# Nyströmformer attention and a SiLU layer on one core: the scores of B and C as 32x32 array tiles

## The chip, the cores and the metric

The kernel runs on one core of one Trainium2 chip. The core has five engines with an instruction queue of their own each: TensorE (PE in the profile, its weight loads PEld), VectorE (DVE), ScalarE (ACT), GpSimd (POOL) and SyncE (SP); DMA queues move data beside them. The metric is the device time in microseconds of one execution, as the median of several runs. Before the change it is 289.93 us (three runs, 289.63 to 290.06).

## The reference

Eight batches, eight heads, 576 rows of 64 values. q and k are averaged over 18 rows each to 32 landmarks. Three softmax matrices follow: A (576x32, q against k's landmarks), B (32x32, landmarks against landmarks) and C (32x576, q's landmarks against k). Z is the inverse of B by six Newton-Schulz steps. The attention A Z C v goes through a layer with a SiLU.

```python
q_lm = q.reshape(B, H, m, S // m, D).mean(axis=3)      # m = 32
k_lm = k.reshape(B, H, m, S // m, D).mean(axis=3)
A = sm(q, k_lm)
Bm = sm(q_lm, k_lm)
C = sm(q_lm, k)
Z = Bm.transpose(0, 1, 3, 2) / (norm_1(Bm) * norm_inf(Bm) + 1e-06)
for _ in range(6):
    Z = 2 * Z - Z @ Bm @ Z
x = A @ Z @ C @ v           # then heads side by side: 4608 x 512
h = x @ w_in                # 512 x 2048
out = (h * sigmoid(h)) @ w_out
```

## The kernel before

The order on every engine is the order of the program text: a manual schedule, each engine executing its instructions in turn. An instruction that waits holds back all that stand behind it on its engine.

**Layout.** Heads go in two quads (g = 0, 1) of four heads; a head's 64 values are kept as 32 partitions times 2 (index e), so a quad fills 128 partitions, and each product with contraction over 64 values is two products (e = 0, 1) that add up. `nat` holds q and k as loaded, in four pieces j (0: q of quad 0, 1: k of quad 0, 2: q of quad 1, 3: k of quad 1), arriving in the order 1, 0, 3, 2. `transpose_qk` (L163, DVE) makes `qkT` of a piece. Landmark sums come from PE with the identity as weights (`landmarks_pe`, L170) for batches 0 to 2, and from five POOL additions (`landmarks_pool`, L183) later; `landmarks_out` (L177) copies PE's sums on ACT into `lmn`.

**Block-diagonal landmarks.** A dense product over 128 partitions mixes four heads, so the weights must be block-diagonal: `bd` (L146) is a 128x128 tile for each piece, zero outside four 32x32 blocks. Batches 0 and 1 (`tiled`) transpose the landmarks into the compact tile `lmc` (`lm_t`, L238), and `bd_expand` (L243) copies the blocks into `bd`. Batches from 2 on write the blocks with four DVE transposes and a fifth for the compact k landmarks `lmk` (`bdiag`, L224).

**Scores.** `b_scores` (L251): sixteen products on 32x32 array tiles from `lmc` in batches 0 and 1, four dense ones from `bd` and `lmk` later. `c_scores(g)` (L360): four dense products of 288 columns with `bd` into a two-bank PSUM tile `scp`. `c_max` (L368, DVE, a maximum and a scaling) and `c_exp` (L377, ACT) follow for each quad, `c_transpose` and `c_out` turn the result on PE in batches 0 and 1, a DMA transpose does it later; `w_scale` (L399) takes the reciprocal of C's row sums, `w_mm` (L405) multiplies with v. A's scores (`a_scores(i)`, L451, three pieces of rows) are dense products with `bd`; `a_max` (DVE) makes the maxima, `a_shift` (L480, PE) adds them to the scores in PSUM, `a_exp` (ACT) and `a_norm` (DVE, then POOL at L497) finish. B goes through `b_max`, `b_exp`, `b_norm` (its transpose `bmt` at L298), `f_mm`, `b_scale`, `f_out` and then `ns_mm` on PE and `ns_step` on DVE in turn, six Newton-Schulz rounds; `x_out`, `z_mm`, `z_out` and `m_unit` (four of them, 64x32 array tiles) give the layer's combined weights `mb`.

**Order.** The first batch's attention runs alone at the start (L597 to L677). Then the main loop goes over the batches: in step s of batch b, `l1(s)` makes layer 1 (four products into one of two two-bank PSUM buffers, the pool `psh`, which `scp` shares), `act(s)` is its SiLU on ACT, and `l2_mm(n)` issues n products of layer 2 from a queue of finished rows. The next batch's attention lies between these, from step d on: d is 6 in batch 0, 3 in batch 1 and 0 later. Step d (step 3 for batch 1) makes the block-diagonal tiles, step d+1 issues `b_scores`, `c_scores(0)` and their maxima, and step d+2 `c_scores(1)`, A's scores, `c_max(1)`, A's maxima, four l2 products, `a_shift(0)` and so on (L741 to L779). In batch 0 no l2 product is queued before step 8.

**Loads.** All loads are issued on POOL, in the order of the text, between POOL's own work; in the start the last w_out loads stand between the Newton-Schulz rounds (L645, L647), and w_in and the first two w_out before everything (L126 to L133).

Of the kernel before, what the change touches and what calls it, by code (L numbers as in the profile page):

```python
# [8 lines left out]
FP = mybir.dt.float32  # L9
BF = mybir.dt.bfloat16  # L10
AF = mybir.ActivationFunctionType
OP = mybir.AluOpType
AX = mybir.AxisListType

# [19 lines left out]
def kernel(  # L36
# [106 lines left out]

    bd_t = []
    for i in range(2):
        z = constp.tile([128, 4, 4 * L, 2], BF, tag=f"bd{i}", name=f"bd{i}")  # L146
        nc.vector.memset(z, 0.0)
        bd_t.append(z)

# [53 lines left out]
    class Att:  # L203
        def __init__(self, b):
            self.b = b
            self.qkT, self.v, self.lmn = qkT_t[b], v_t[b], lmn_t[b]
            self.bd = bd_t[b % 2]


            self.tiled = b < 2  # L210
            self.by_dma = b >= 2
            if self.tiled:
                self.lmc = attp.tile([128, 4, L, 2], BF, tag="lmc", name="lmc")
            else:
                self.lmk = attp.tile([128, 2, L, 2], BF, tag="lmk", name="lmk")
            self.bb = None
            self.m_done = 0
            self.csum = attp.tile([128, 2], FP, tag="csum", name="csum")
            self.eCT, self.t = [None, None], [None, None]
            self.s, self.sa, self.w = [None, None], [None] * 3, [None, None]  # L220
            self.fx = None


        def bdiag(self, gs=(0, 1)):  # L224
            j0, j1 = 2 * gs[0], 2 * gs[-1] + 2
            for h in range(4):
                p = slice(32 * h, 32 * h + 32)
                nc.vector.transpose(
                    out=self.bd[p, j0:j1, 32 * h:32 * h + 32, :]
                        .rearrange("p j l e -> p j (l e)").bitcast(FP),  # L230
                    in_=self.lmn[p, j0:j1, :].bitcast(FP))
            n = len(gs)
            nc.vector.transpose(
                out=self.lmk[:, gs[0]:gs[0] + n, :, :].rearrange("p g l e -> p (g l e)").bitcast(FP),
                in_=self.lmn.rearrange("p (g j) d -> p g j d", j=2)
                    [:, gs[0]:gs[0] + n, 1, :].bitcast(FP))

        def lm_t(self, g):  # L238
            nc.vector.transpose(
                out=self.lmc[:, 2 * g:2 * g + 2].rearrange("p j l e -> p (j l e)").bitcast(FP),  # L240
                in_=self.lmn[:, 2 * g:2 * g + 2, :].bitcast(FP))

        def bd_expand(self, g, *copy):  # L243
            for h in range(4):
                p = slice(32 * h, 32 * h + 32)
                copy[h % len(copy)](
                     out=self.bd[p, 2 * g:2 * g + 2, 32 * h:32 * h + 32, :],
                     in_=self.lmc[p, 2 * g:2 * g + 2])


        def b_scores(self):  # L251
            self.bb = psn1("bb")
            self.sb = self.bb[:, 448:512]
            if self.tiled:
                for g in range(2):
                    for e in range(2):
                        for h in range(4):
                            p = slice(32 * h, 32 * h + 32)
                            mm(self.sb[p, 32 * g:32 * g + 32], self.lmc[p, 2 * g, :, e],
                               self.lmc[p, 2 * g + 1, :, e], start=(g == 0 and e == 0),  # L260
                               stop=(e == 1))
                return
            for g in range(2):
                for e in range(2):
                    mm(self.sb[:, 32 * g:32 * g + 32], self.bd[:, 2 * g, :, e],
                       self.lmk[:, g, :, e], start=(g == 0 and e == 0), stop=(e == 1))

        def b_max(self):
            s2 = sc / (SEG * SEG)
# [87 lines left out]
            self.fx = n  # L357


        def c_scores(self, g):  # L360
            self.s[g] = ps2("scp")
            for hf in range(2):
                for e in range(2):
                    mm(self.s[g][:, hf, 0:HF], self.bd[:, 2 * g, :, e],
                       self.qkT[:, 2 * g + 1, HF * hf:HF * hf + HF, e],
                       start=(e == 0), stop=(e == 1))

        def c_max(self, g):  # L368
            mx = attp.tile([128, 1], FP, tag="cmx", name="cmx")
# [28 lines left out]

        def w_scale(self):  # L399
            self.wsc = attp.tile([128, 2], FP, tag="wsc", name="wsc")  # L400
            nc.vector.reciprocal(out=self.wsc, in_=self.csum)  # L401
            nc.vector.tensor_tensor(out=self.wsc, in0=self.wsc, in1=self.nrm, op=OP.mult)


        def w_mm(self):  # L405
            vv = self.v.rearrange("p h (c d) -> p h c d", d=Dh)
            self.w = psa1("wp")[:, 0:2 * Dh].rearrange("p (g d) -> p g d", d=Dh)
            for g in range(2):
                for c in range(VC):
                    for h in range(4):  # L410
                        p = slice(32 * h, 32 * h + 32)
                        mm(self.w[p, g, :], self.eCT[g][0:VP, c, p], vv[:, 4 * g + h, c, :],
                           start=(c == 0 and g == 0), stop=(c == VC - 1))

        def w_out(self):
# [35 lines left out]
        def a_scores(self, i):  # L451
# [8 lines left out]
            for c in range(2 * i, min(2 * i + 2, len(TCH))):  # L460
# [3 lines left out]
                for g in range(2):  # L464
                    for e in range(2):
                        mm(ov[:, g].rearrange("p r (j l) -> p r j l", l=L),
                           self.qkT[:, 2 * g, c0:c1, e],
                           self.bd[:, 2 * g + 1, :, e].rearrange("p (j r l) -> p r j l", r=2, l=L),
                           start=first, stop=(e == 1))
                        first = False  # L470

# [131 lines left out]
    a = Att(0)  # L603
    landmarks_pe(0, lp, 3, 1)
    a.lm_t(0)
    a.bd_expand(0, nc.scalar.copy)
    transpose_qk(0, 3)
    landmarks_pe(0, lp, 2, 1)
    transpose_qk(0, 2)
    landmarks_out(0, lp, 2, 2)  # L610
    a.lm_t(1)
    a.b_scores()
    a.bd_expand(1, nc.vector.tensor_copy, nc.scalar.copy)
    a.c_scores(0)
    a.b_max()
    a.b_exp()
    a.a_start()
    a.a_scores(0)
    a.c_max(0)
    a.c_exp(0)  # L620
    a.b_norm()
    a.f_mm()
    a.a_scores(1)
    a.b_scale()
    a.f_out()
    a.ns_mm()
    a.c_scores(1)
    a.a_max(0)
    a.ns_step()
    a.ns_mm()  # L630
# [4 lines left out]
    a.ns_mm()  # L635
    a.a_scores(2)
    a.a_shift(1)
    a.c_max(1)
    a.c_exp(1)
    a.a_exp(1)  # L640
    a.ns_step()
    a.ns_mm()
# [38 lines left out]
    for b in range(B):  # L681
# [14 lines left out]
        for s in range(NDC):  # L696
            if b > 1 and s in (0, 4) and a0.m_done < 4:
                a0.m_unit(a0.m_done)
            if b < 2 and s < 4:
# [13 lines left out]
                if b == 0 and s == 0:  # L713
# [1 line left out]
                    a0.a_out(1)  # L715
                    a = Att(1)
                    a.lm_t(0)
                    a.bd_expand(0, nc.gpsimd.tensor_copy)
                if s == 1 and b == 0:
                    landmarks_out(1, lp, 2, 2)  # L720
                    a.lm_t(1)
                    a.bd_expand(1, nc.gpsimd.tensor_copy)
                if s == 3 and b == 1:
                    landmarks_out(2, lp, 0, 4)
                    a = Att(2)
                    a.bdiag()
                l2_mm(cnt[s])
            elif b == 0 and s < 7:
                l1(s)
# [5 lines left out]

            elif s == d:
                l1(s)
                a.bdiag()
                act(s)
                l2_mm(cnt[s])  # L740
            elif s == d + 1:  # L741
                l1(s)
                a.b_scores()
                a.c_scores(0)
                a.b_max()
                a.c_max(0)
                act(s)
                table(AF.Exp)
                a.b_exp()
                l2_mm(cnt[s])  # L750
            elif s == d + 2:
                a.c_scores(1)
                a.a_start()
                a.a_scores(0)
                a.a_scores(1)
# [156 lines left out]
```

## Time and profile before

| | us |
|---|---|
| median of three runs | 289.93 |
| the profiled execution | 288.62 |
| its span in the profile | 286.4 |
| PE busy | 263.8 |
| ACT busy | 176.8 |
| DVE busy | 162.2 |
| POOL busy | 110.8 |
| layer 2 products (ops), 576 of them, busy | 148.1 |
| layer 1 products (hps), 512, busy | 83.0 |
| C's score products (scp), 64, busy | 12.1 |
| bdiag's transposes, 24 and 6 | 7.2 and 1.5 |

The span is what the profile records between the first and the last instruction of the execution; the time of a run has some 2.2 us around it. Products on PE overlap, so that busy times of groups are no sums of what each costs; two rows' starts show what lies between. The page's slices of PE's granted clock read 9 nearly throughout, with an 8 in slice 4 (from 21 us) and a 7 in slice 10 (from 64 us).

### The profile page before, as it was taken

What the parts mean: (1) busy time and instruction counts of PE and PEld (TensorE: products, weight loads), DVE (VectorE), ACT (ScalarE), POOL (GpSimd) and SP (SyncE); (2) the same over time, 40 slices, a digit from 0 to 9 for tenths busy, and PEclk for the clock granted to TensorE, in tenths of its full rate; (3) what the DMA queues carried; (4) which work ended last, traced back from release to release, by engine and by line L of the source; (5) the groups of instructions that cost most, each with busy time, mean ns of one, the idle gap of its engine ahead of it and who ended that gap; (6) DMA issues with size and microseconds to landing.
All of it is one profiled execution on the core that took longest, in us unless ns stands there. A gap on an engine that the chain in (4) does not pass through costs nothing.

```text
span 286.4 us, 6289 instructions
## 1 busy us (share of the span) xinstructions
PE 263.8 (92%) x2520; PEld 149.3 (52%) x2520; DVE 162.2 (57%) x396; ACT 176.8 (62%) x349; POOL 110.8 (39%) x139
## 2 busy tenths in 40 slices
PE   1787898997999899999899999999899999999994
PEld 1645555564554555455454655465545555456541
DVE  4896786376676754857676764856694652200000
ACT  2456686575756875669566865678566945646511
POOL 8335533213099409941597029710991030000000
PEclk9998999997999999999999999999999999999999
DMA  6999999916746874619494929203470603020012
GB/s 110 202 208 208 206 207 211 189 39 110 148 65 134 167 129 66 144 61 177 95 152 91 182 62 143 94 37 94 57 143 37 92 20 98 37 76 37 37 73 74
DMA packets 37788, 32.31 MB, mean 113 GB/s; under 512 B 18816, under 2 KB 29056, under 8 KB 37760
## 3 DMA queue, kind: packets, MB, share of 16 engines
q0 software_dynamic: 15104, 18.35, 39.4%
q1 hardware_dynamic: 22656, 13.57, 18.4%
q8 instruction: 19, 0.31, 0.5%
q14 instruction: 9, 0.07, 0.1%
HBM read 36.70 MB, written 9.44 MB: 161 GB/s over the span
## 4 chain that ended last, share of the span: by engine, by line
PE 76%; DVE 11%; POOL 5%; DMA 2%; ACT 2%; issue 1%; DVEq 0%; POOLq 0%; ACTq 0%
PE ops L72 40%; PE hps L72 18%; PE bb L72 5%; PE mp L72 4%; PE scp L72 3%; PE sa L72 3%; DMA nat<-in_q_dram 2%; DVE arec L495 2%; POOL lma L189 2%; PE lmp L72 1%; DVE fx L354 1%; DVE mb L538 1%; PE wp L72 1%; DVE cmx L370 1%; DVE arec L496 1%
## 5 line engine op out<-in xcount | busy, mean ns | idle before, releaser
L72 PE MATMUL ops<-w_out_sb,gT 128*128 128x512 bf16 x576 | 148.1, 382 | 0.1
L563 ACT ACTIVATE gT<-hps 128x576 bf16<-128x576 f32 x128 | 82.3, 650 | 60.0 <-PE hps L72 59.7
L72 PE MATMUL hps<-AT,mb 128*128 128x288 bf16 x512 | 83.0, 288 | 1.0 <-ACT gT L563 0.4
L72 PEld LDWEIGHTS <-gT 128*128 128x128 bf16 x576 | 51.9, 98 | 47.7 <-issue 6.5
L72 PEld LDWEIGHTS <-mb 128*128 128x128 bf16 x512 | 47.8, 98 | 27.0 <-issue 2.5
L497 POOL TENSOR_TENSOR an<-ex,arec 128x512 bf16<-128x512 bf16 (+1 forms) x24 | 21.4, 902 | 80.7 <-DVE wsc L401 38.3
L167 DVE STREAM_TRANSPOSE qkT<-nat 128x576 f32<-128x576 f32 x32 | 39.6, 1247 | 1.6 <-DMA nat<-in_k_dram 1.3
L538 DVE CAST mb<-mp 128x512 bf16<-128x512 f32 x32 | 22.1, 690 | 20.1 <-PE mp L72 19.7
L354 DVE SCALAR_TENSOR_TENSOR fx<-fx,bb 128x320 bf16<-128x320 bf16 (+2 forms) x48 | 18.3, 382 | 26.4 <-PE bb L72 26.2
L587 ACT COPY ost<-ops 128x512 f32<-128x512 f32 x36 | 21.0, 585 | 16.3 <-PE ops L72 15.2
L189 POOL TENSOR_TENSOR lma<-nat 128x1152 f32<-128x1152 bf16 x10 | 23.8, 2376 | 0.0
L140 ACT ACT_TABLE_LOAD x16 | 20.5, 1283 | 1.1 <-PEq L896 0.8
L539 ACT CAST mb<-mp 128x512 bf16<-128x512 f32 x32 | 18.7, 583 | 4.0 <-PE mp L72 4.0
L72 PEld LDWEIGHTS <-ident 128*128 128x128 bf16 (+1 forms) x240 | 12.3, 110 | 12.8 <-issue 5.3
L72 PE MATMUL lmp<-nat,ident 128*128 128x64 bf16 x216 | 11.0, 213 | 6.8 <-DMA nat<-in_k_dram 6.2
L72 PEld LDWEIGHTS <-fx 32*32 32x32 bf16 (+1 forms) x168 | 7.8, 95 | 16.1 <-DVE fx L354 7.3
L72 PE MATMUL bb<-fx 32*32 32x64 bf16 (+2 forms) x168 | 13.4, 211 | 2.9 <-DVE fx L354 2.5
L567 POOL COPY gT<-gT 128x1024 bf16<-128x1024 bf16 x4 | 4.1, 1036 | 30.0 <-ACT gT L563 30.0
L370 DVE TENSOR_REDUCE cmx<-scp 128x1 f32<-128x576 f32 x16 | 12.1, 757 | 4.9 <-PE scp L72 4.4
L495 DVE TENSOR_REDUCE arec<-ex 128x16 f32<-128x512 bf16 (+1 forms) x24 | 14.0, 585 | 0.0
L378 ACT ACTIVATE eC<-scp,cbs 128x576 bf16<-128x576 f32 x16 | 11.7, 740 | 3.6 <-DVE cbs L373 2.2
L488 ACT ACTIVATE ex<-sa 128x512 bf16<-128x512 f32 (+1 forms) x17 | 9.9, 584 | 6.2 <-PE sa L72 6.2
(82 smaller groups left out, 252.0 us busy)
## 6 DMA issues: line engine op xcount, KB each, us to landing
out_dram<-ost SPq DMA_DIRECT2D x36, 256.0 KB, 2.2
nat<-in_k_dram POOLq DMA_DIRECT2D x16, 288.0 KB, 6.2
nat<-in_q_dram POOLq DMA_DIRECT2D x16, 288.0 KB, 7.4
v<-in_v_dram POOLq DMA_DIRECT2D x8, 576.0 KB, 6.7
w_in_sb<-in_moe_w_in_dram POOLq DMA_DIRECT2D x4, 512.0 KB, 14.9
w_out_sb<-in_moe_w_out_dram POOLq DMA_DIRECT2D x4, 512.0 KB, 16.9
AT<-an SPq DMA_TRANSPOSE x30, 4.1
eCT<-eC SPq DMA_TRANSPOSE x12, 4.4
```

The lines of the kernel that those rows point to most:

```text
L72: nc.tensor.matmul(out=o, lhsT=lhsT, rhs=rhs, start=start, stop=stop, skip_group_check=True)
L140: nc.scalar.activation(out=spare[:, 1:2], in_=spare[:, 0:1], func=func)
L167: nc.vector.transpose(out=o.rearrange("p (l t) -> p t l", t=SEG), in_=nat_t[b][:, j, :].bitcast(FP).rearrange("p (t l) -> p t l", l=L))
L189: nc.gpsimd.tensor_tensor(out=a1, in0=nat[:, :, 0:3 * w], in1=nat[:, :, 3 * w:6 * w], op=OP.add)
L354: nc.vector.scalar_tensor_tensor(out=n[:, :, lo:], in0=self.fx[:, :, lo:], scalar=2.0, in1=self.p[:, :, lo:], op0=OP.mult, op1=OP.subtract)
L370: nc.vector.tensor_reduce(out=mx, in_=self.s[g][:, :, 0:HF], op=OP.max, axis=AX.XY, negate=True)
L495: nc.vector.tensor_reduce(out=r, in_=x, op=OP.add, axis=AX.X)
L497: nc.gpsimd.tensor_tensor(out=self.an[0:pr, c:c + n, :].rearrange("p c (h l) -> p (c h) l", l=L), in0=x, in1=r.unsqueeze(2).to_broadcast(( ...
L538: nc.vector.tensor_copy(out=o[:, 0, :], in_=m[0])
L539: nc.scalar.copy(out=o[:, 1, :], in_=m[1])
L563: nc.scalar.activation(out=gT_t[b][:, 2 * s:2 * s + 2, o:o + HF], in_=h[:, :, 0:HF], func=AF.Silu)
L587: nc.scalar.copy(out=ost, in_=st["ps"])
```

## The change

B's and C's scores use the compact landmarks `lmc` in every batch, on 32x32 array tiles. C's second quad writes its heads two quadrants away (`quadrant`: head h of quad 1 to partitions 32*(h^2)), and both quads' products are issued alternately, four and four. `bd` keeps only k's landmarks, for A, and is half as large. The rows of C in quad 1 being swapped by halves, `w_mm` reads `eCT` at the swapped place, and `w_scale` takes its reciprocals in three instructions. `bdiag` gives way to one `lm_t` over four pieces and four `bd_expand` copies on DVE.

The orders move too. In the loop, step d+1 now issues l1, act, l2, and then B's scores and both C quads, and step d+2 starts with A's scores. In the start, C's first quad with its maximum and exponential comes between the last two landmark sums; the last transpose (piece 2) moves from before B's scores to behind `f_mm`; `bd_expand` is half on POOL and half on ACT, behind `b_exp`; C's second quad, its maximum and its exponential come before B's norm and A's scores.

```diff
-        z = constp.tile([128, 4, 4 * L, 2], BF, tag=f"bd{i}", name=f"bd{i}")
+        z = constp.tile([128, 2, 4 * L, 2], BF, tag=f"bd{i}", name=f"bd{i}")
...
-        def bdiag(self, gs=(0, 1)):
...
-        def lm_t(self, g):
+        def lm_t(self, g, n=1):
             nc.vector.transpose(
-                out=self.lmc[:, 2 * g:2 * g + 2].rearrange("p j l e -> p (j l e)").bitcast(FP),
-                in_=self.lmn[:, 2 * g:2 * g + 2, :].bitcast(FP))
-
-        def bd_expand(self, g, *copy):
+                out=self.lmc[:, 2 * g:2 * g + 2 * n].rearrange("p j l e -> p (j l e)").bitcast(FP),
+                in_=self.lmn[:, 2 * g:2 * g + 2 * n, :].bitcast(FP))
+
+        def bd_expand(self, g, n, *copy):
             for h in range(4):
                 p = slice(32 * h, 32 * h + 32)
                 copy[h % len(copy)](
-                     out=self.bd[p, 2 * g:2 * g + 2, 32 * h:32 * h + 32, :],
-                     in_=self.lmc[p, 2 * g:2 * g + 2])
+                     out=self.bd[p, g:g + n, 32 * h:32 * h + 32, :],
+                     in_=self.lmc[p].rearrange("p (g j) l e -> p g j l e", j=2)[:, g:g + n, 1])
...
-                    mm(self.sb[:, 32 * g:32 * g + 32], self.bd[:, 2 * g, :, e],
-                       self.lmk[:, g, :, e], start=(g == 0 and e == 0), stop=(e == 1))
+                    for h in range(4):
+                        p = slice(32 * h, 32 * h + 32)
+                        mm(self.sb[p, 32 * g:32 * g + 32], self.lmc[p, 2 * g, :, e],
+                           self.lmc[p, 2 * g + 1, :, e], start=(g == 0 and e == 0),
+                           stop=(e == 1))
...
-        def c_scores(self, g):
-            self.s[g] = ps2("scp")
+        def quadrant(self, g, h):
+            h = h ^ (2 * g)
+            return slice(32 * h, 32 * h + 32)
+
+        def c_scores(self, gs=(0, 1)):
+            for g in gs:
+                self.s[g] = ps2("scp")
             for hf in range(2):
                 for e in range(2):
-                    mm(self.s[g][:, hf, 0:HF], self.bd[:, 2 * g, :, e],
-                       self.qkT[:, 2 * g + 1, HF * hf:HF * hf + HF, e],
-                       start=(e == 0), stop=(e == 1))
+                    for g in gs:
+                        for h in range(4):
+                            p = slice(32 * h, 32 * h + 32)
+                            mm(self.s[g][self.quadrant(g, h), hf, 0:HF],
+                               self.lmc[p, 2 * g, :, e],
+                               self.qkT[p, 2 * g + 1, HF * hf:HF * hf + HF, e],
+                               start=(e == 0), stop=(e == 1))
...
-            nc.vector.reciprocal(out=self.wsc, in_=self.csum)
+            nc.vector.reciprocal(out=self.wsc[:, 0:1], in_=self.csum[:, 0:1])
+            for r in range(2):
+                nc.vector.reciprocal(out=self.wsc[64 * r:64 * r + 64, 1:2],
+                                     in_=self.csum[64 - 64 * r:128 - 64 * r, 1:2])
...
     a.lm_t(0)
-    a.bd_expand(0, nc.scalar.copy)
+    a.c_scores((0,))
     transpose_qk(0, 3)
+    a.c_max(0)
+    a.c_exp(0)
     landmarks_pe(0, lp, 2, 1)
-    transpose_qk(0, 2)
     landmarks_out(0, lp, 2, 2)
     a.lm_t(1)
     a.b_scores()
-    a.bd_expand(1, nc.vector.tensor_copy, nc.scalar.copy)
-    a.c_scores(0)
+    a.c_scores((1,))
     a.b_max()
     a.b_exp()
+    a.bd_expand(0, 2, nc.gpsimd.tensor_copy, nc.scalar.copy)
+    a.c_max(1)
+    a.b_norm()
+    a.c_exp(1)
     a.a_start()
+    a.f_mm()
+    transpose_qk(0, 2)
     a.a_scores(0)
-    a.c_max(0)
-    a.c_exp(0)
-    a.b_norm()
-    a.f_mm()
-    a.a_scores(1)
     a.b_scale()
     a.f_out()
     a.ns_mm()
-    a.c_scores(1)
+    a.a_scores(1)
     a.a_max(0)
...
     a.a_shift(1)
-    a.c_max(1)
-    a.c_exp(1)
     a.a_exp(1)
...
-                    a.bdiag()
+                    a.lm_t(0, 2)
+                    a.bd_expand(0, 2, nc.vector.tensor_copy)
...
             elif s == d + 1:
                 l1(s)
+                act(s)
+                l2_mm(cnt[s])
                 a.b_scores()
-                a.c_scores(0)
+                a.c_scores()
                 a.b_max()
                 a.c_max(0)
-                act(s)
                 table(AF.Exp)
                 a.b_exp()
-                l2_mm(cnt[s])
             elif s == d + 2:
-                a.c_scores(1)
                 a.a_start()
```

In the loop, batch 1's `bd_expand` (two calls in steps 0 and 1 of batch 0) stays on POOL and copies one piece instead of two for each quad.

More of the change, by code (lines that the diff above doesn't have):

```diff
@@ L211, in __init__ @@
             self.by_dma = b >= 2
[L212 to L215, printed above, removed]
+            self.lmc = attp.tile([128, 4, L, 2], BF, tag="lmc", name="lmc")
             self.bb = None
@@ L221, in __init__ @@
             self.fx = None
-        def bdiag(self, gs=(0, 1)):
[L225 to L236, printed above, removed]
-        def lm_t(self, g):
-            nc.vector.transpose(
-                out=self.lmc[:, 2 * g:2 * g + 2].rearrange("p j l e -> p (j l e)").bitcast(FP),
-                in_=self.lmn[:, 2 * g:2 * g + 2, :].bitcast(FP))
-        def bd_expand(self, g, *copy):
+        def lm_t(self, g, n=1):
+            nc.vector.transpose(
+                out=self.lmc[:, 2 * g:2 * g + 2 * n].rearrange("p j l e -> p (j l e)").bitcast(FP),
+                in_=self.lmn[:, 2 * g:2 * g + 2 * n, :].bitcast(FP))
+        def bd_expand(self, g, n, *copy):
             for h in range(4):
@@ L253, in b_scores @@
             self.sb = self.bb[:, 448:512]
[L254 to L262, printed above, removed]
             for g in range(2):
                 for e in range(2):
-                    mm(self.sb[:, 32 * g:32 * g + 32], self.bd[:, 2 * g, :, e],
-                       self.lmk[:, g, :, e], start=(g == 0 and e == 0), stop=(e == 1))
+                    for h in range(4):
[3 more added lines that the diff above has]
+                           stop=(e == 1))
         def b_max(self):
@@ L411, in w_mm @@
                         p = slice(32 * h, 32 * h + 32)
-                        mm(self.w[p, g, :], self.eCT[g][0:VP, c, p], vv[:, 4 * g + h, c, :],
+                        mm(self.w[p, g, :], self.eCT[g][0:VP, c, self.quadrant(g, h)], vv[:, 4 * g + h, c, :],
                            start=(c == 0 and g == 0), stop=(c == VC - 1))
@@ L467, in a_scores @@
                            self.qkT[:, 2 * g, c0:c1, e],
-                           self.bd[:, 2 * g + 1, :, e].rearrange("p (j r l) -> p r j l", r=2, l=L),
+                           self.bd[:, g, :, e].rearrange("p (j r l) -> p r j l", r=2, l=L),
                            start=first, stop=(e == 1))
@@ L717 @@
                     a.lm_t(0)
-                    a.bd_expand(0, nc.gpsimd.tensor_copy)
+                    a.bd_expand(0, 1, nc.gpsimd.tensor_copy)
                 if s == 1 and b == 0:
@@ L721 @@
                     a.lm_t(1)
-                    a.bd_expand(1, nc.gpsimd.tensor_copy)
+                    a.bd_expand(1, 1, nc.gpsimd.tensor_copy)
                 if s == 3 and b == 1:
@@ L737 @@
                 l1(s)
-                a.bdiag()
+                if b > 1:
+                    a.lm_t(0, 2)
+                    a.bd_expand(0, 2, nc.vector.tensor_copy)
                 act(s)
```

## The prediction

> **What bounds the kernel now.** I read first the page's busy rows, then the chain that ended last, then the table of who waited for whom, and last the timeline of four places where this edit works: the start, and the changes to the second, third and seventh batch. In the first row TensorE is busy 263.8 of 286.4 us and no other engine passes 62%: from 27 us on, what makes PE wait or adds PE time is paid in full. The last three rows say where PE still waits.
>
> ```profile
> PE 263.8 (92%) x2520; PEld 149.3 (52%) x2520; DVE 162.2 (57%) x396; ACT 176.8 (62%) x349; POOL 110.8 (39%) x139
> ...
> PE lmp L72 <- DMA nat<-in_k_dram: 6.2, 2, 5.6
> PE bb L72 <- DVE lmk L233: 2.8, 2, 1.9
> PE bb L72 <- DVE fx L354: 2.5, 4, 0.9
> ```
>
> The timeline of the start (start, duration, engine, line, instruction, in brackets the idle time before and its releaser). Until about 27 us no layer 1 exists to fill PE: the path runs through landmarks, B's scores (bb<-lmc), B's norm, six Newton-Schulz rounds and z. POOL's rows are the other thing to see: it issues the loads in order, and each w_out issue waits for an earlier load to land.
>
> ```profile
> 10.21 1.12 PE L72 MATMUL lmp<-nat,ident 128*128 128x64 bf16 x18 [0.33 <-DMA nat<-in_q_dram]
> 11.37 0.27 ACT L180 CAST lmn<-lmp 128x128 bf16<-128x128 f32 x1 [1.40 <-PE lmp L72]
> 11.69 0.52 PE L72 MATMUL bb<-lmc 32*32 32x32 bf16 x16 [0.35 <-ACT lmn L180]
> 14.63 0.24 DVE L298 STREAM_TRANSPOSE bmt<-bm 128x64 bf16<-128x64 bf16 x1
> 16.20 0.29 PE L72 MATMUL bb<-fx 32*32 32x64 bf16 x8
> 18.99 0.74 POOL L122 DMA_DIRECT2D w_out_sb<-in_moe_w_out_dram  x1 [2.40 <-DMA w_in_sb<-in_moe_w_in_dram]
> 24.27 0.25 PE L72 MATMUL bb<-xb,W 128*64 128x64 bf16 x4 [1.05 <-DVE xb L286]
> ```
>
> The change to the third batch: DVE makes both block-diagonal tiles late, PE waits 1.91 us, and then four l2 products take 1.88 instead of the usual 1.02 us. The granted clock is 0.50 from 68 to 70 us and 0.79 from 70 to 72.
>
> ```profile
> 66.80 0.27 PE L72 MATMUL bb<-lmk,bd 128*128 128x32 bf16 x4 [1.91 <-DVE lmk L233]
> 67.42 1.88 PE L72 MATMUL ops<-w_out_sb,gT 128*128 128x512 bf16 x4
> 72.21 0.38 PE L72 MATMUL sa<-nm,ident 128*128 128x512 bf16 x1
> ```
>
> A later change (to the seventh batch): no wait, C's quads lie apart, four l2 products between them.
>
> ```profile
> 190.21 0.26 PE L72 MATMUL bb<-lmk,bd 128*128 128x32 bf16 x4
> 190.31 0.67 PE L72 MATMUL scp<-qkT,bd 128*128 128x288 bf16 x4
> 191.68 0.67 PE L72 MATMUL scp<-qkT,bd 128*128 128x288 bf16 x4
> 192.39 0.76 DVE L370 TENSOR_REDUCE cmx<-scp 128x1 f32<-128x576 f32 x1 [0.43 <-PE scp L72]
> 193.99 0.38 PE L72 MATMUL sa<-nm,ident 128*128 128x512 bf16 x1
> ```
>
> **The price of a tiled score.** A dense C quad costs PE 0.51 us (190.31 to the next product at 190.82), both 1.02; dense B costs 0.10 (190.21 to 190.31). Tiled B, at 36.92 us, holds PE 0.20 (sixteen products). Entering and leaving the tiled mode: a step with m_unit lasts 1.80 us (147.08 to 148.88 in the chain), one without 1.35 (125.88 to 127.23); of the 0.45, one stream of 512 columns is 0.215 (0.86 for four), so the two switches cost 0.235. Tiled C is 4 rounds of 8 products. If a round is one stream of 288 columns (0.12), C costs 0.48; if the quads don't overlap, 8 rounds, 0.96. m_unit runs eight products of 512 columns in that 0.215, so eight tiles over two PSUM banks do overlap; I take 0.55, with 0.07 for the last round's staggered starts. B and C thus cost 0.20 + 0.55 + 0.235 = 0.99 against 1.12: 0.13 gained, where nothing else waits.
>
> One rule speaks against that. Four heads of one quad write one bank here. The Newton-Schulz row has four heads in one bank too: its first result reaches DVE 0.29 us after the start (46.98 to 47.27), where one after the other the eight streams of 64 columns would alone need about 0.21 on top of the usual latency. The Trainium skill, TensorEngine Tiling (Array Packing), Gotcha 1: PSUM Pressure, says that different row tiles cannot use one bank at the same time. By that rule C would go two at a time, 16 x 0.12 = 1.92 us, about 1.4 more in each of seven stages, near 10 us on the sum; by the row it costs nothing, and I follow the row.
>
> **A stage of batches 3 to 6 (four of them).** Moved: act(s) and the four l2 products before B, both C quads together. Now from l1 (189.72) to the first a_shift (193.99) is 4.27, PE never idle. After: l1 0.48, l2 0.86, switch in 0.10, B 0.20, C 0.55 = 2.19. Then DVE takes two c_max in a row and a_max. The start of the second batch already shows this: cmx at 37.85, the next at 38.71, a_max 39.56, a_shift at 40.30, so 2.45 from the first c_max. The first c_max follows PE's last score by 0.20 (190.82 to 191.02). 2.19 + 0.20 + 2.45 = 4.84. PE itself needs only switch out 0.14, A's scores 0.92 and l2 0.88 = 1.94 of that 2.65, and stands 0.7 us at a_shift. Behind it in PE's queue lie the third A score, l2 and layer 1; nothing else is late there to take it up. Loss 0.55 a stage, 2.2 in all; bounds 0.48 (C at 0.48) and 0.98 (C at 0.96). On DVE five transposes (1.48) become one of about 0.3 and four copies of 0.18, all under PE's work; uncovered they would cost at most the 1.91 us that bdiag costs in the third batch. The second batch's POOL copies (four of 0.29 for each quad, now half as wide) lie under layer 1; uncovered, 1.2 us.
>
> **Third batch.** DVE ends its transposes at 65.25, lm_t is done at 65.55. PE: l1 64.23, l2 to 65.57, B from 65.67: the 1.91 us wait is gone, so I take the clock's fall as gone too (a wait of 0.87 at 95.53 brought none, and the new stall is 0.9). Expansion ends about 66.3, then b_max, c_max from 66.75, a_shift 66.75 + 2.45 = 69.2 against 72.21: gain 3.0. Bounds 1.9 (the wait alone) and 3.9 (no stall). **Fourth batch.** The 0.87 us wait goes: l1 to a_shift was 5.30 (94.01 to 99.31), becomes 4.84: gain 0.5. **Second batch.** act(7) has no l2 to hide it: C's second quad needs its buffer, free at 37.75; 37.75 + 0.55 + 0.20 + 2.45 = 40.95 against 40.30: loss 0.6.
>
> **The start.** (a) C's first quad is set between the last two landmark sums; products there are slow (scp x4 1.14 at 12.14, 0.67 at 190.31), so PE is busy with it from 9.8 to about 11.0 and the last landmarks end 12.1 instead of 11.33. (b) ACT's copy of them now queues behind c_exp(0), which waits for c_max(0): 11.1 + 0.95 + 0.95 = 13.0, so B's scores start at 13.6 instead of 11.69, 1.9 late. (c) From there to bmt one C quad lies in between, as before: bmt ends 16.8. (d) The last transpose_qk, idle time at 10.20 before, now stands between b_norm and b_scale: 1.26, then the same 1.24 (14.91 to 16.15): f_out at 19.3. (e) Half of bd_expand goes to POOL, and in POOL's order behind the w_out issue at 18.99, paced by loads: 18.99 + 0.74 + two copies of 0.29 = 20.35. A's first scores wait for it, and the first Newton-Schulz product stands behind them on PE: 20.4 + 0.9 = 21.3 against 16.20, 5.1 late. (f) From there to z the old 8.07 us lose a C quad's c_max (0.86) on DVE and c_exp on ACT; A's second scores take the C quad's place on PE. I take 0.7 off: z comes 4.4 late. Bounds: 5.1 (nothing off) and 1.3: without (e) 1.9 + 1.26 - 0.7 = 2.5, less 1.2 if the spell at clock 0.64 (27 to 31 us) goes, in which four hps took 1.37 instead of 0.66 and eighteen landmark products 1.17 instead of 0.69. Three reciprocals for one in w_scale: 2 x 0.15, within that. The smaller memsets end before the first load lands.
>
> **Sum.** 4.4 + 0.6 - 3.0 - 0.5 + 2.2 = +3.7 us. The profiled execution took 288.62 us (span 286.4 and 2.2 around it) and lies 1.3 under the median of 289.93: 292.3 there, 293.6 as a median.
>
> **Rivals.** Quads that run one after the other: 0.41 more in seven stages, +2.9: 296.5. For it: no row shows two different moving operands in one head's row strip with weights changed every round; against it m_unit. 0.10. POOL's copies not held: only (e) falls, start 2.5 late, sum +1.8: 291.7; for it, POOL has nothing but issues there, against it the order of its queue. 0.15, of which 0.05 ends within no change. The other side: DVE's chain doesn't hold a_shift. Then a stage is 2.19 + 1.94 = 4.13, gain 0.14 x 4, third batch 3.9, fourth 1.2, second 0.3 lost: 4.4 + 0.3 - 3.9 - 1.2 - 0.6 = -1.0: 288.9. It decides as soon as the stall falls from 0.7 below 0.1; for it, the first quad's products come first in each round; against it, 2.45 was measured. 0.15. That the edit does not do what it says I count as the first rival.
>
> **How the numbers follow.** Mine has 0.60: 293.6, own range 291.5 (c_max and c_exp both off the start's 5.1: 3.5; third batch 3.9; stages 0.48) to 295.4 (start 5.1, third batch 1.9). Faster by over 0.2% (about what a measurement of this kernel can tell from no change) is the last rival, 0.15; within it 0.05; slower 0.80. The range runs from 290.0 (the POOL rival, 291.7, less the clock's 1.2 and 0.07 for C in seven stages) to 296.8, just past the first rival; the last rival alone, and what lies beyond 296.8, stay out.
>
> **What would show it.** Right: bb<-fx first at 21 us, sa<-bd first at 20.4 released by POOL, ops at 65 us with no half clock, PE idle 0.7 before sa<-nm in late stages, the waits on lmk gone. Wrong: a first bb<-fx before 19, no such idle time, or scp taking 0.9 us of PE a batch.

## The result and the profile after

The changed kernel takes 300.76 us as the median of four runs (298.23 to 301.68), the kernel before 289.78 us in four runs (286.77 to 290.06): a ratio of 1.0387, 95% interval 1.0328 to 1.0446. It is slower by 11 us where the forecast said 3.7, and lies outside the range of 290.0 to 296.8. The profiled execution took 301.68 us with a span of 300.0, against 288.62 and 286.4; it is the slowest of the four, so that what is accounted for below is 13.9 us and not 11.

The busy row of the page and the head of the table of who waited for whom, by PE (total, times, longest, in us):

```profile
PE 262.9 (88%) x2748; PEld 148.1 (49%) x2784; DVE 163.8 (55%) x410; ACT 176.4 (59%) x345; POOL 110.9 (37%) x141
```

```profile
PE bb L76 <- DVE fx L336: 8.4, 8, 1.9
PE lmp L76 <- DMA nat<-in_k_dram: 6.7, 2, 5.6
PE sa L76 <- DVE nm L470: 4.4, 7, 0.8
PE sa L76 <- POOL bd L234: 4.0, 1, 4.0
```

PE is busy 0.9 us less in a span 13.6 us longer. Busy time is not work, though: up to step 8 of batch 0 PE is busy 36.4 us where it was 31.4, because its products take longer there ("Wrong, second step" below), and from there on 226.5 where it was 232.4. The wait on lmk is gone as forecast. Two waits were forecast, sa on POOL's bd and sa on DVE's nm (0.5 to 0.8 in seven stages). The largest one was not: bb on fx, 8.4 us, was 2.5.

To find where each microsecond went, I compared the start of every layer 1 step (hps) in the two profiled executions. The difference after minus before grows like this:

| place | forecast | measured |
|---|---|---|
| first layer 1 | +4.4 | +7.03 |
| from there to step 7 of batch 0 | 0 | +2.23 |
| change to the second batch | +0.6 | +0.53 |
| third | -3.0 | -3.09 |
| fourth | -0.5 | -0.56 |
| fifth to eighth, together | +2.2 | +1.89 (0.46 to 0.48 each) |
| a later step in each of batches 1 to 6 | 0 | +5.87 (six times 0.98) |
| sum | +3.7 | +13.9 |

The terms of the stages stand. Two things are wrong: the start, and a loss that the forecast doesn't have, always five steps behind the new scores.

**The stages as they are now.** The timeline at the third batch (start, duration, engine, line, instruction; in brackets the idle time before and its releaser), and at the seventh:

```profile
75.47 0.23 PE L76 MATMUL bb<-lmc 32*32 32x32 bf16 x9
78.94 0.38 PE L76 MATMUL sa<-nm,ident 128*128 128x512 bf16 x1 [0.80 <-DVE nm L470]
```

```profile
200.71 0.65 PE L76 MATMUL hps<-AT,mb 128*128 128x288 bf16 x4
202.16 0.47 PEld L76 LDWEIGHTS <-lmc 32*32 32x32 bf16 x48 [0.42 <-issue]
202.28 0.67 PE L76 MATMUL scp<-qkT,lmc 32*32 32x288 bf16 x28
202.88 1.10 PE L76 MATMUL sa<-bd,qkT 128*128 128x128 bf16 x16
203.00 0.76 DVE L362 TENSOR_REDUCE cmx<-scp 128x1 f32<-128x576 f32 x1
203.87 0.75 DVE L362 TENSOR_REDUCE cmx<-scp 128x1 f32<-128x576 f32 x1
205.45 0.38 PE L76 MATMUL sa<-nm,ident 128*128 128x512 bf16 x1 [0.61 <-DVE nm L470]
```

At the third batch B's scores follow layer 2 without a wait. At the seventh, B and both C quads, 48 products, hold PE from 202.16 to 202.88, and DVE's first c_max starts 0.12 later. From l1 to a_shift it is 4.74 us (200.71 to 205.45; forecast 4.84, before 4.27), with PE idle 0.61 at the end (forecast 0.7) behind two c_max and a_max.

**The start.** The timeline:

```profile
13.61 0.49 PE L76 MATMUL bb<-lmc 32*32 32x32 bf16 x12 [1.07 <-ACT lmn L184]
16.44 0.24 DVE L280 STREAM_TRANSPOSE bmt<-bm 128x64 bf16<-128x64 bf16 x1
19.51 0.74 POOL L126 DMA_DIRECT2D w_out_sb<-in_moe_w_out_dram  x1 [1.47 <-DMA w_in_sb<-in_moe_w_in_dram]
20.25 0.64 POOL L234 COPY bd<-lmc 32x128 bf16<-32x128 bf16 x2
20.94 1.01 PE L76 MATMUL sa<-bd,qkT 128*128 128x128 bf16 x8 [3.97 <-POOL bd L234]
21.89 0.29 PE L76 MATMUL bb<-fx 32*32 32x64 bf16 x8
30.66 0.47 PE L76 MATMUL bb<-xb,W 128*64 128x64 bf16 x4
```

POOL's two copies do stand behind the w_out issue, which waits for an earlier load, and A's first scores wait 3.97 us for them. The first Newton-Schulz product comes at 21.89 against 16.20: 5.69 late (forecast 5.1). From there to z it is 8.77 us where it was 8.07, and from z to the first layer 1 3.39 where it was 2.75.

**The loss that was not forecast.** The same place on either side, DVE's and POOL's rows around w_scale; the kernel before first, then the changed one:

```profile
78.73 0.25 DVE L496 RECIPROCAL arec<-arec 128x16 f32<-128x16 f32 x1
78.90 0.11 DVE L401 RECIPROCAL wsc<-csum 128x2 f32<-128x2 f32 x1
79.04 0.16 DVE L402 TENSOR_TENSOR wsc<-wsc,nrm 128x2 f32<-128x2 f32 x1
79.13 1.04 POOL L497 TENSOR_TENSOR an<-ex,arec 128x512 bf16<-128x512 bf16 x1 [10.99 <-DVE wsc L401]
80.00 0.43 DVE L354 SCALAR_TENSOR_TENSOR fx<-fx,bb 128x320 bf16<-128x320 bf16 x1
```

```profile
85.43 0.25 DVE L491 RECIPROCAL arec<-arec 128x16 f32<-128x16 f32 x1
85.60 0.10 DVE L393 RECIPROCAL wsc<-csum 128x1 f32<-128x1 f32 x1
85.72 0.33 DVE L395 RECIPROCAL wsc<-csum 64x1 f32<-64x1 f32 x2
85.83 1.04 POOL L492 TENSOR_TENSOR an<-ex,arec 128x512 bf16<-128x512 bf16 x1 [7.84 <-DVE arec L491]
86.08 0.81 DVE L397 TENSOR_TENSOR wsc<-wsc,nrm 128x2 f32<-128x2 f32 x1
87.69 0.43 DVE L336 SCALAR_TENSOR_TENSOR fx<-fx,bb 128x320 bf16<-128x320 bf16 x1
88.17 0.31 PE L76 MATMUL bb<-fx 128*128 128x160 bf16 x2 [1.06 <-DVE fx L336]
```

A multiply of 128x2 numbers takes 0.16 us before and 0.81 after. Before, it starts 0.09 us ahead of POOL's a_norm multiply, which arec has released (the row names wsc, but POOL starts 0.15 us behind the end of arec in both kernels). After, the two added reciprocals put it 0.25 us behind, and it ends where POOL's ends (86.89 and 86.87). The next ns_step on DVE starts 2.01 us behind the end of arec instead of 1.02, and PE, which did not wait there before, waits 1.06. The multiply's start is 0.34 us later and its length 0.65 more, together the 0.98 that the table has six times.

### The profile page after: what moved, and what is told of

The parts are those of the page before. It is cut to its first block, busy times and chain, and to the rows that moved or that the text cites. A ratio compares the mean times of both kernels' runs of the same rounds, so it can differ in the third digit from the quotient of the medians.

```text
span 300.0 us, 6795 instructions
## 1 busy us (share of the span) xinstructions
PE 262.9 (88%) x2748; PEld 148.1 (49%) x2784; DVE 163.8 (55%) x410; ACT 176.4 (59%) x345; POOL 110.9 (37%) x141
## 4 chain that ended last, share of the span: by engine, by line
PE 72%; DVE 15%; DMA 5%; issue 3%; ACT 2%; POOL 2%; POOLq 0%; DVEq 0%; ACTq 0%
PE ops L76 36%; PE hps L76 19%; PE bb L76 5%; DMA w_in_sb<-in_moe_w_in_dram 5%; PE mp L76 4%; DVE cmx L362 3%; DVE arec L490 3%; PE sa L76 2%; PE lmp L76 2%; DVE fx L336 2%; DVE wsc L397 2%; PE wp L76 1%; DVE nm L470 1%; PE scp L76 1%; DVE mb L533 1%
## 5 line engine op out<-in xcount | busy, mean ns | idle before, releaser
L76 PE MATMUL ops<-w_out_sb,gT 128*128 128x512 bf16 x540 | 140.9, 380 | 3.6 <-issue 2.4
L76 PE MATMUL hps<-AT,mb 128*128 128x288 bf16 x512 | 84.7, 292 | 0.8 <-DVE mb L533 0.3
L76 PEld LDWEIGHTS <-mb 128*128 128x128 bf16 x512 | 48.5, 99 | 27.9 <-issue 2.5
L76 PEld LDWEIGHTS <-ident 128*128 128x128 bf16 (+1 forms) x240 | 13.6, 117 | 13.8 <-issue 5.6
L76 PE MATMUL lmp<-nat,ident 128*128 128x64 bf16 x216 | 12.4, 225 | 7.0 <-DMA nat<-in_k_dram 6.7
L76 PEld LDWEIGHTS <-qkT 128*128 128x128 bf16 (+1 forms) x160 | 10.2, 104 | 14.3 <-issue 14.1
L76 PE MATMUL mp<-w_in_sb,zwT 64*32 64x512 bf16 x256 | 14.0, 414 | 0.0
```

Source lines behind the costliest of these rows:

```text
L76: nc.tensor.matmul(out=o, lhsT=lhsT, rhs=rhs, start=start, stop=stop, skip_group_check=True)
```

## The experiments

Offsets below are, as in the table, the start of a layer 1 step in the profiled execution less that of the kernel before. The kernels of 1 to 4, of 5 to 8 and of 9 to 11 each share their runs of the kernel before; ratios are to it, with 95% intervals.

**1. One reciprocal again.**

```diff
-            nc.vector.reciprocal(out=self.wsc[:, 0:1], in_=self.csum[:, 0:1])
-            for r in range(2):
-                nc.vector.reciprocal(out=self.wsc[64 * r:64 * r + 64, 1:2],
-                                     in_=self.csum[64 - 64 * r:128 - 64 * r, 1:2])
+            nc.vector.reciprocal(out=self.wsc, in_=self.csum)
```

> The changed kernel with w_scale's three reciprocals put back to one; the swap of the halves in the second quad's scales is left out. Theory A (collision): in the changed kernel the small multiply of w_scale takes 798 ns in the median instead of 161 because the two extra reciprocals (0.16 us each) let it start after POOL's multiply of a_norm has begun. Without them it takes about 160 ns again, PE's waits on fx of about 1 us in each of batches 1 to 6 go, and the kernel is 5.9 us (6 x 0.98) faster than the changed one, near 295. Theory B (the longer stage before it makes DVE late): the waits stay but for the 0.3 us of the two reciprocals, at most 1.9 us faster, 299 or more. The start stays 7.0 us late by both.

295.58 us, ratio 1.0151 [1.0122, 1.0180]. The row of the tile wsc (least, median and longest duration in ns):

```profile
L394 DVE TENSOR_TENSOR wsc<-wsc,nrm x8: 160/161/162, 28.1 to 239.0; 128x2 f32<-128x2 f32 x8
```

All six steps of 0.98 are gone (offset at the end 7.63 instead of 13.89); the start is unchanged at 7.03.

**2. The reciprocals kept, w_scale moved ahead of a_norm(0).**

```diff
                 if s == d + 4:
-                    a.a_norm(0)
                     a.w_scale()
+                    a.a_norm(0)
                     a.a_norm(1)
```

> The changed kernel with w_scale, three reciprocals and all, moved ahead of a_norm(0) in the main loop, so that its multiply ends before POOL's a_norm multiply can begin. Theory A (collision): the multiply is short again, DVE is later by 0.6 us a batch instead of 1.3; waits on fx fall from about 1 us to 0.3 or less, 4 to 5.9 us faster than the changed kernel. Theory B (the number of instructions on DVE counts, wherever they stand): same time as the changed kernel within 1 us.

296.03 us, ratio 1.0181 [1.0121, 1.0240]. The multiply's median is 161 ns again with all three reciprocals in place, and the step costs 0.34 a batch instead of 0.98. So the reciprocals' own time is a third of the loss and the meeting with POOL two thirds. This execution, whose start is the same (6.99), has no further loss up to step 7 (6.95): the 2.23 us of the changed kernel's table there are not in every execution.

**3. The kernel before, with its reciprocal cut in three and nothing else.**

```diff
-            nc.vector.reciprocal(out=self.wsc, in_=self.csum)
+            nc.vector.reciprocal(out=self.wsc[:, 0:1], in_=self.csum[:, 0:1])
+            for r in range(2):
+                nc.vector.reciprocal(out=self.wsc[64 * r:64 * r + 64, 1:2],
+                                     in_=self.csum[64 * r:64 * r + 64, 1:2])
```

> The kernel before, with w_scale's reciprocal in three instructions of the same sizes as in the change (no swap). Theory A (collision): its multiply starts 0.34 us later, after POOL's a_norm multiply has begun, and takes some 0.8 us in batches 1 to 6; 0.98 us lost in each, 5.9 us slower than before, near 295.7. Theory B (the stage order is to blame): 0.3 us of DVE work in batches in which DVE was not late, 0 to 1 us slower.

296.45 us, ratio 1.0178 [1.0147, 1.0210]: five us by two small instructions in a kernel without any of the change's scores. The timeline and the tile:

```profile
81.25 1.04 POOL L500 TENSOR_TENSOR an<-ex,arec 128x512 bf16<-128x512 bf16 x1 [11.01 <-DVE arec L499]
81.38 0.92 DVE L405 TENSOR_TENSOR wsc<-wsc,nrm 128x2 f32<-128x2 f32 x1
83.59 0.31 PE L72 MATMUL bb<-fx 128*128 128x160 bf16 x2 [1.06 <-DVE fx L354]
```

```profile
L405 DVE TENSOR_TENSOR wsc<-wsc,nrm x8: 160/915/931, 23.4 to 238.6; 128x2 f32<-128x2 f32 x8
```

Again the multiply starts inside POOL's row and ends with it (82.30 and 82.29), and 0.98 is lost in each of six batches. Another 2.1 us are lost at the start.

**4. The old order of the start in the changed kernel** (all of the diff's lines of the first batch undone, with C's quads as tiles in their old places).

```diff
-    a.c_scores((0,))
+    a.bd_expand(0, 1, nc.scalar.copy)
...
-    a.bd_expand(0, 2, nc.gpsimd.tensor_copy, nc.scalar.copy)
...
-    a.ns_mm()
-    a.a_scores(1)
+    a.ns_mm()
+    a.c_scores((1,))
```

> The changed kernel with the first batch's order as it was before (C's quads at their old places, the last transpose ahead of B, bd_expand on ACT and DVE for each quad when its landmarks are there), scores still tiled. Theory: the new order of the start costs 7.0 us up to the first layer 1 product, and the slow products until 44 us another 2.2; the old one gives all of it back: 9 us faster than the changed kernel, near 291.5. Rival: tiled products themselves are slow in the start, or the load order paces it: less than 4 us come back. In the trace the first layer 1 product starts at 27 us by the theory and after 31 by the rival.

295.93 us, ratio 1.0184 [1.0137, 1.0230]. The first layer 1 is 0.10 late instead of 7.03: the start's loss is the new order's. The spell behind it, in which products run at about half their rate, did not go: 1.9 us more are lost by step 4 of batch 0 (the kernel before has such a spell too, with a granted clock of 0.57 from 26 to 30 us; here it is 0.50 from 26 to 34). With experiment 1 this accounts for the result, within the intervals: 1.0387 less the 0.0236 that experiment 1 takes off and the 0.0203 of this one is 0.995.

**5. The new start, with POOL's copies given to ACT.**

```diff
-    a.bd_expand(0, 2, nc.gpsimd.tensor_copy, nc.scalar.copy)
+    a.bd_expand(0, 2, nc.scalar.copy)
```

> The changed kernel with all four bd_expand copies of the first batch on ACT, none on POOL. Theory: A's first scores and behind them the first Newton-Schulz product wait 4.0 us for POOL's two copies, which queue behind two paced w_out issues; on ACT they wait for the last transpose alone (about 18.0 us): A's first scores 2.9 us earlier than 20.94, the first layer 1 product near 31 instead of 34.05, about 3 us faster than the changed kernel, near 297. Rival: DVE's chain (transpose, B's scale) sets the end anyway: less than 1 us.

297.90 us, ratio 1.0270 [1.0214, 1.0326]. A's first scores start at 16.16, the first Newton-Schulz product at 18.17 instead of 21.89, and the first layer 1 is 3.30 late: 3.7 of the 7.0 us are POOL's queue.

**6. The fifth kernel, with the transpose back at its old place.**

```diff
     landmarks_pe(0, lp, 2, 1)
+    transpose_qk(0, 2)
     landmarks_out(0, lp, 2, 2)
...
     a.f_mm()
-    transpose_qk(0, 2)
```

> The same, and the last transpose of the first batch back at its old place, ahead of the landmarks' copy. Theory: its 1.26 us leave the path between B's norm and its scale; the first Newton-Schulz product comes 1.2 us earlier than with the copies on ACT alone, the first layer 1 product near 30, some 2.8 us after that of the kernel before: what is left is the landmarks' copy queued on ACT behind C's first exponential (1.9 us) and C's quad on PE. Near 296. Rival: A's scores, which need this transpose, hold the path at the same place: no gain over the copies on ACT alone.

298.32 us, ratio 1.0248 [1.0168, 1.0328]; the first layer 1 is 2.89 late, 0.4 better where 1.2 was expected. The transpose behind f_mm was nearly free: back in its old place it holds up lm_t(1), and B's scores start at 13.37 instead of 12.86. In the profiled execution a later loss of 1.64 us, where the granted clock fell to 0.56 behind a wait of 1.91 us on fx, hides the gain; the medians of the two experiments can't be told apart.

**7. Three more layer 2 products ahead of the first a_shift, in the changed kernel**, to fill the 0.6 us in which PE waits for nm.

```diff
-                l2_mm(4)
+                l2_mm(7)
                 a.a_shift(0)
...
-                l2_mm(cnt[s] - 6)
+                l2_mm(cnt[s] - 9)
```

(The table of counts gives step d+2 three more and three later steps one less each.)

> The changed kernel with three more l2 products ahead of the first a_shift in each stage, taken from steps 8 to 10 of the batch. Theory: PE stands 0.6 to 0.8 us there for DVE's two c_max and a_max; three products (0.65 us) fill it, and the stage costs 0.14 us less than before the change instead of 0.47 more: 0.6 x 7 = 4.2 us faster than the changed kernel, near 296.5. Rival: the wait moves to the next a_shift, whose maximum is late as well: less than 1.5 us.

301.78 us, ratio 1.0396 [1.0341, 1.0451]: no gain. The waits on nm are gone, but others have grown:

```profile
PE bb L76 <- DVE fx L336: 9.2, 8, 1.9
...
PE ops L76 <- ACT ost L582: 1.6, 1, 1.6
```

In batch 1 the products moved ahead themselves wait 1.6 us for ACT's copies, and they are missing where w_scale's multiply makes PE wait for fx: that wait is 1.87 us instead of 1.06. The fx waits of the later batches are as long as without the cover. Two fx waits are followed by a fall of the granted clock (0.61 at 89 to 92 us in batch 1, 0.56 at 215 to 218 in batch 5); the second costs 1.59 us. So the cover did work where nothing else happened: the offsets of batches 2, 3, 4 and 6 grow by 0.36 to 0.38 less than in the changed kernel, the change to the second batch by 0.65 less. Batch 1 (2.56 more) and the fall in batch 5 take this back.

**8. Old start, reciprocals early, and the cover.** The three reciprocals move to step d+3, behind b_scale, and only the multiply stays at w_scale's place.

```diff
                 a.b_scale()
+                a.w_rec()
                 a.f_out()
...
-                    a.w_scale()
+                    a.w_scale(rec=False)
```

> The changed kernel with the old start, w_scale's three reciprocals early (behind b_scale, where DVE waits for PE) and only its multiply at the old place, and three more l2 products ahead of the first a_shift. Theory: the multiply ends before POOL begins, so nothing is lost in batches 1 to 6; the third batch's gain of 3.1 to 3.9 and the fourth's of 0.6 to 1.2 stand, the four later stages are 0.1 better than before the change: 4 to 5.5 us faster than the kernel before, near 285. Rival: tiled scores give nothing once the stall is covered, since what is left over is lost again at a later wait: within 1.5 us of before.

286.64 us, ratio 0.9881 [0.9826, 0.9937]: the first version faster than both kernels, by less than the 4 to 5.5 us expected. The multiply's median is 97 ns, and the offset at the end is -2.87.

**9. The same without the cover.**

```diff
-                l2_mm(7)
+                l2_mm(4)
```

> The changed kernel with the old order of the start and with the three reciprocals issued early (behind b_scale, so that only the multiply is left at w_scale's old place), but without the extra layer 2 products ahead of the first a_shift that the last repaired kernel had (286.64 us, 2.87 us under before at the end of the profiled execution). Theory (the collision with POOL's multiply and the new start make up the whole loss; the four terms of the stages were right): start within 0.3 us of before, up to 1 more while its products run slow, then +0.5 in the second batch, -3.1 in the third, -0.6 in the fourth, +0.5 in each of the next four: about -1.2 us, near 288.5 us, and the w_scale multiply takes under 0.2 us. The cover is then worth about 1.7 us. Rival (the cover is worthless, as it was in the changed kernel): 286.6 us as with it.

287.87 us, ratio 0.9958 [0.9923, 0.9994], and an offset of -1.21 at the end where -1.2 was expected. The second, third and fourth batch read +0.54, -3.09 and -0.57, the later stages +0.46 to +0.47. That the sum meets -1.2 is luck all the same: the start with its slow products has lost 0.93 by step 7 of batch 0, which the -1.2 leaves out, and nearly as much is won at w_scale's place in batches 1 to 6 (0.21, 0.21, 0.21, 0.03, 0.22 and 0.03), which was not forecast. These 0.91 us lie where the reciprocals were taken away and not at the scores; the kernel before with early reciprocals was not run. The cover is worth 1.66 us in the profiles (-2.87 against -1.21): 0.37 in each of batches 2 to 6, as in experiment 7, 0.65 at the change to the second batch and 0.04 at the start, less 0.88 lost in batch 1.

**10. The cover in all batches but batch 1.**

```diff
-                l2_mm(7)
+                l2_mm(4 if b == 1 else 7)
```

> The last repaired kernel with the extra layer 2 products in every batch but batch 1, where four go ahead of the first a_shift as in the changed kernel: there the extra products had waited 1.6 us for ACT. Theory (in that batch the cover's products wait longer than what they cover): about 1 us faster than with the cover in all batches, 285.6 us; the wait of ops for ACT's ost is gone. Rival (the wait only moves to the next product that needs the same copy): no change, 286.6 us.

286.19 us, ratio 0.9877 [0.9822, 0.9932]; against experiment 8 the intervals overlap, so the time decides nothing. In the profiles batch 1 gains 0.87 us (from its step 4 to step 1 of the next batch the offset changes by -3.29, in experiment 8 by -2.42). But the wait of ops on ACT is not gone: it comes in the next batch's stage, at 99.43 us, with 0.72 instead of 1.59 us, and 0.64 of the gain is left at the end. Theory and rival each hold in part. The profiled execution lost more than that at its start (1.05 us against experiment 8), where w_scale's first multiply took 1.96 us (last section).

**11. The ninth kernel with the loop's old order:** the two C quads in different steps.

```diff
-                a.c_scores()
+                a.c_scores((0,))
...
             elif s == d + 2:
+                a.c_scores((1,))
                 a.a_start()
```

> The kernel without cover (first of this set), with the old order in the loop's steps: B's scores and C's first quad ahead of the SiLU and of layer 2, C's second quad one step later, so that the quads are not issued together and the array changes its mode twice. Theory (tiled quads cost about half when they are issued side by side, and each pair of mode switches costs 0.235 us): each quad alone takes 0.48 us, both 0.96 instead of 0.55, and the stall of 0.6 us at a_shift goes with C's second maximum off the chain: within 0.3 us a stage of the kernel without cover, near 288.5 us; PE's two C rows hold it 0.4 to 0.5 us each. Rival 1 (quads cost the same apart, 0.27 each): 0.5 us a stage less, 285.5 us. Rival 2 (a quad alone is slower still, its four row strips sharing banks, 0.96 each): 1 us a stage more, 293 us or above.

287.56 us, ratio 0.9932 [0.9907, 0.9956], not to be told from experiment 9. PE's rows of a late stage, first of this kernel, then of the ninth:

```profile
189.49 0.67 PE L76 MATMUL scp<-qkT,lmc 32*32 32x288 bf16 x16
190.33 0.81 PE L76 MATMUL ops<-w_out_sb,gT 128*128 128x512 bf16 x3 [0.16 <-issue]
191.07 0.69 PE L76 MATMUL scp<-qkT,lmc 32*32 32x288 bf16 x16
191.69 1.10 PE L76 MATMUL sa<-bd,qkT 128*128 128x128 bf16 x16
```

```profile
189.37 0.68 PE L76 MATMUL scp<-qkT,lmc 32*32 32x288 bf16 x28
189.97 1.10 PE L76 MATMUL sa<-bd,qkT 128*128 128x128 bf16 x16
192.54 0.38 PE L76 MATMUL sa<-nm,ident 128*128 128x512 bf16 x1 [0.61 <-DVE nm L474]
```

One quad alone holds PE 0.62 us (191.07 to 191.69); both together hold it 0.60 (189.37 to 189.97), or 0.65 with four of their products that the trace has from 189.32 on, among B's. The second quad is all but free when it is issued beside the first, and the array time saved is real: from step 8 of batch 0 on PE is busy 226.0 us in the ninth kernel and 228.8 in this one. (Over the whole span it is 258.0 and 262.5; the rest of the difference is the start, where this execution's products ran slow for longer.) A late stage still costs the same (+0.46 and +0.42 against before), because without the pairing no stall at a_shift is left to be seen: the paired order ends in DVE's two c_max and a_max, the old one in PE.

## Why the prediction was right in direction and wrong in size

**Right, by its own steps.** The tiled scores were sized well: 0.20 and 0.55 for B and C, a mode switch besides, measured 0.72 for both with 48 loads, and the rival in which the quads go one after the other is refuted by experiment 11 and by the 0.60 us of the pair. The rule of the Trainium skill that was set aside (TensorEngine Tiling (Array Packing), Gotcha 1: PSUM Pressure) would have made C 1.92 us by the prediction's estimate; the trace does not agree with it here. The stall of 0.7 at a_shift is 0.61, with the chain that was named: two c_max, then a_max. The rival in which DVE's chain does not hold a_shift is gone with it. The second, third and fourth batch are within 0.1 us, the later stages 0.08 each below. Of the start, (a) to (c) hold: B's scores at 13.61 (13.6), bmt ending at 16.68 (16.8); the transpose of (d) stands where it was said, and experiment 6 prices it at 0.4 and not 1.26 on this path. So does (e): POOL's copies stand behind the w_out issue, and experiment 5 gets 3.7 us by taking them away from there.

**Wrong, first step: "Three reciprocals for one in w_scale: 2 x 0.15, within that".** It costed two instructions by their own duration, and only at the start, as lying within that range. They are issued in every batch, ahead of a multiply that had 0.09 us to spare before POOL's a_norm. Behind POOL, the multiply waits for it, ns_step waits for the multiply and PE for ns_step: 0.98 in each of six batches, 5.87 in all. Experiment 3 shows it without the rest of the change, experiment 1 takes it away, and experiment 2 shows that it is the meeting with POOL and not the reciprocals alone. Both signs were to be read in the profile of before. The rows at 79.04 and 79.13 give the margin, and the tile's durations gave the price, 160 ns at least and 1178 at most, the longest at the start beside POOL's work. The Trainium skill says why (SBUF — State Buffer, Who interferes with whom): a DVE instruction with two SBUF inputs and a GpSimd one that reads SBUF exclude each other, and the later one waits for the whole of the earlier one. The ends, 86.89 beside 86.87 and 82.30 beside 82.29, agree.

**Wrong, second step: (f), "I take 0.7 off: z comes 4.4 late".** (e) was 0.6 short, 0.5 of it because the w_out issue itself came at 19.51 instead of 18.99. Then nothing came off: the loop to z took 0.70 more and the way to the first layer 1 0.64 more, 7.03 in all. The instructions named in (f) did leave the path, but PE ran that stretch at half rate. The same six products inside the Newton-Schulz rounds, in the kernel before and in the changed one:

```profile
19.76 0.54 PE L391 MATMUL ctp<-ident,eC 128*96 128x128 bf16 x6
```

```profile
25.67 0.88 PE L383 MATMUL ctp<-ident,eC 128*96 128x128 bf16 x6
```

The windows (stretch, length, PE busy with its instructions, granted clock, share and rate of the DMAs) of the kernel before, then of experiment 2, whose start is the changed kernel's:

```profile
18.00:22.00 4.00, 3.59 (x60) 1.00 1.16 206
22.00:26.00 4.00, 2.44 (x96) 1.00 1.16 212
```

```profile
18.00:22.00 4.00, 1.07 (x16) 0.50 1.15 206
22.00:26.00 4.00, 3.78 (x50) 0.50 1.15 208
26.00:30.00 4.00, 3.69 (x94) 0.50 1.24 207
30.00:34.00 4.00, 3.55 (x54) 0.50 1.25 207
```

In the changed kernel's own profile the record of the clock reads 1.00 there, but its products take the same time as in experiment 2 (the first A scores 1.01 us for eight, the six products above 0.88), so I read its rate from these. The kernel before is slow at first as well, though its record reads 1.00: its a_shift takes 0.61 us at 17.72 and at 19.04, later 0.38. It is at the full rate from about 19.5 us to 26, and this is what the changed kernel lacks. That the half rate took back the 0.7 is read from these rows; it was not tried by itself. The forecast priced the clock only where it might gain, 1.2 for the spell from 27 us on; it had a PE that idles 4 us and did not ask what follows. The long wait alone is not the cause: experiment 5 has no wait above 1.7 us from B's scores to z and ran at half rate too (the six products 0.88 us). Nor does it help that PE is busy again: in experiment 2 it is busy 3.55 to 3.78 of each 4 us from 22 to 34 us, and the clock stays at 0.50. What brings the full rate back is not shown.

**What stays open** is the 2.23 us between the first layer 1 and step 7 of batch 0. Experiments 2 and 7 have the same start and none of it, experiment 1 the same start and 1.9; experiments 4, 5 and 11 have about 2, experiments 8 and 9 about 1. The products there run at half rate for a while longer or shorter from one execution to the next, and nothing here shows what decides it.

## What to carry to other kernels

Before a small instruction is added to an engine's queue, look at what stands right behind it and by how little that is ahead of its neighbours: here 0.3 us of reciprocals cost 5.9, because the next multiply lost a margin of 0.09 us to another engine. A group whose longest duration is seven times its median can tell of such a meeting in the profile of before; find the row and what ran beside it. And when an order is improved on one engine, the gain is kept only if the stall it leaves (here at a_shift) gets work that is not already the cover of something else, as the moved products were in batch 1.

## What the runs showed of the hardware that was not expected

**The multiply can wait for more than POOL's arithmetic.** In the tenth kernel w_scale's first multiply, of 128x2 numbers, took 1.96 us. DVE's row, then POOL's:

```profile
21.45 1.96 DVE L401 TENSOR_TENSOR wsc<-wsc,nrm 128x2 f32<-128x2 f32 x1
```

```profile
21.63 1.06 POOL L496 TENSOR_TENSOR an<-ex,arec 128x512 bf16<-128x512 bf16 x1
22.63 0.80 POOL L126 DMA_DIRECT2D w_out_sb<-in_moe_w_out_dram  x1
```

It ends at 23.41, with POOL's DMA issue (23.43) and not with POOL's multiply (22.69), which began after it. The kernel before has the same at its start: the multiply from 21.79 to 22.97, POOL's issue to 22.98, POOL's multiply to 22.24. In the ninth kernel POOL's multiply has ended (22.08) when DVE's begins. The w_out issue stands beside it, and it takes 0.81 us where it takes 0.10 in most later batches:

```profile
22.15 0.81 DVE L401 TENSOR_TENSOR wsc<-wsc,nrm 128x2 f32<-128x2 f32 x1
```

```profile
22.01 0.80 POOL L126 DMA_DIRECT2D w_out_sb<-in_moe_w_out_dram  x1
```

Experiments 4, 8 and 11 have it at the same place. Not every issue does this: the changed kernel's first multiply ends at 29.21 with POOL's multiply (29.19), while an issue of v goes on to 29.99. What sets the two apart is not shown.

**The granted clock fell to about 0.6 for some 3 us behind waits of PE of 1.9 us**, in experiments 6 and 7 as in the third batch of the kernel before, and not behind other waits of that length (the changed kernel waits 1.91 us at 150 and at 215 us, and its table shows no loss there beyond the 0.98; experiment 7 waits as long at 149 us without a fall). A fall cost 1.64 us in experiment 6 and 1.59 in batch 5 of experiment 7; in the kernel before, the way from B's scores to a_shift takes 5.41 us (66.80 to 72.21) in the third batch and 3.78 in the seventh. So such a wait may cost nearly twice its own length.
